# Attention and two MoE layers on one core: raw weight pieces fetched apart from their conversion, and new places for the start-up's steps

## The chip, the cores and the metric

The program runs on one core of a Trainium2 chip. Its time is device microseconds (us) of one launch; lower is better. The core has five instruction engines, each of which takes its own queue in order: PE (TensorE: matmuls and transposes), DVE (VectorE), ACT (ScalarE), POOL (GpSimd) and SP (SyncE, which issues most of the DMAs here). SBUF is the on-chip memory, PSUM the accumulators that PE writes.

## The reference

Attention with four batches, eight heads, 576 tokens and head size 64; then a dense MoE layer on the 2304 tokens; then a layer of eight experts of which each token takes one.

```
scores = q @ k.T / 8                       # (4, 8, 576, 576)
heads 0..3: keep 0 <= i - j < 32;  heads 4..7: keep j <= i and j % 32 == i % 32
x = softmax(scores) @ v                    # -> (2304, 512)
h = x @ w_in                               # 512 -> 1024      (float64 weights)
solu = h * softmax(h)
y = layernorm(solu) * g_ln @ w_out         # 1024 -> 512      (float64 weights)
logits = y @ w_gate + modality_bias[modality_id]
e = argmax(logits);  out = softmax(logits)[e] * (relu(y @ w1[e]) @ w2[e])
```

## The kernel before, in words

The big matmuls split each float32 operand into a high part and a low rest and add three products. So each weight matrix stands in SBUF twice: `winH` and `winL` for `w_in`, `woH` and `woL` for `w_out`.

`w_in` and `w_out` arrive as float64. A **raw piece** is 128 rows of 512 such numbers (512 KB); there are eight of either matrix. One piece is converted in steps. A multiplication of its upper words gives `mag` (on ACT or on POOL, by the letter in `MAG_ON`). Three operations on DVE put the bits of a float32 together in `wf` (lines 246, 247, 249); with a `P` in `SIGN_ON`, POOL clears all but the sign bit first (line 242) and two operations on DVE are enough (243, 249). ACT copies the high part (257 for `w_in`, 269 for `w_out`), and DVE or POOL subtracts it to get the low part (258; 272 and 274 by `LOW_ON`). A piece of `w_out` then goes through `fuse_gate`: four transposes of `wf` (`pt`) and four small matmuls with the gate's weights (`pg`). When all eight are done, `column_sums` runs 32 matmuls on them.

Attention works on pairs of heads, sixteen in all, with batch 0's strided pairs first. A pair has four **units**. A unit of a strided pair in batch 0 (`compact`) goes: 16 small matmuls into the PSUM tile `S`; DVE adds the mask, takes the maximum, subtracts it; ACT takes the exponential; DVE sums and inverts (396); four POOL operations spread the result into a zeroed tile (`spread`, line 399); PE transposes it (`pP`, 510), ACT copies that (`pT`, 518), and after two units PE multiplies with the values (`po`, 526), which ACT and DVE split into `xTH` and `xTL`. Units 0 to 7 are of this kind; units 8 to 15, two local pairs, take another way with the normalisation `ex` on POOL (462). Before a pair's units its q and k are transposed on PE (`ptq`) and copied by ACT (`qT`, `kz`).

`attention_slots` cuts this into numbered slots; `take(n)` emits them up to number n. Ahead of the first MoE tile the program takes some 72 slots, with the conversions of `w_in` set between them by `W_IN_AT`. Within the eighteen tiles of the first MoE layer, `between` emits conversions of `w_out` (`W_OUT_AT`), gates (`GATE_AT`) and slots of the next batch (`TAKES`). A tile has `moe_a` (24 matmuls of 512 columns into two `ph` tiles, then the exponential `e` on ACT and `so` on DVE, line 643, which frees `ph`) and, one tile later, `moe_b`. A tile scheduler orders each engine's queue from that. All buffers of a tag rotate: an instruction that fills one waits for the last reader of what it held. `raw` has three buffers, and q and k of the pairs share three of the tag `qk`.

Of the kernel before, what the change touches and what calls it, by code (L numbers as in the profile page):

```python
# [28 lines left out]
def tile_attention_moe_moe2(  # L29
# [56 lines left out]
    TAKES = [0, 5, 1, 8, 1, 0, 7, 0, 0, 4, 2, 0, 3, 0, 6, 0, 1, 0, 4, 0, 3, 0, 6, 0, 5, 0, 7, 0, 2, 1, 0, 3, 4, 2, 5, 0, 3, 0, 2, 0, 0, 0, 5, 0, 7, 0, 0, 4, 1, 0, 5, 2, 0, 0, 1, 1, 4, 0, 5, 0, 4, 0, 2, 0, 2, 0, 6, 4, 2, 2, 3, 0, 3, 0, 4, 0, 0, 1, 2, 1, 0, 0, 12, 0, 8, 3, 1, 0, 2, 2, 0, 0, 4, 0, 4, 0, 3, 0, 6, 0, 1, 1, 4, 0, 0, 0, 0, 0, 0]  # L86
# [46 lines left out]
    def flip_tile(out_, in_, eye):  # L133
        return nc.tensor.transpose(out_, in_, eye)  # L134
# [5 lines left out]
    def warm(n):  # L140
        wide = ident.bitcast(mybir.dt.bfloat16)
        for _ in range(n):
            nc.tensor.matmul(warm_out, wide[:, 0:P], wide, start=True, stop=True)
# [6 lines left out]

    def build_masks():
        nc.gpsimd.memset(rebias, 2.0 ** -112)
        nc.gpsimd.memset(zeros, 0.0)
        rank = mp.tile([P, 1], I32, name="rank", tag="e")
        rankf = mp.tile([P, 1], F32, name="rankf", tag="e")
# [6 lines left out]
        place = mp.tile([P, WIN], F32, name="place", tag="so")  # L162
        early = mp.tile([P, WIN], F32, name="early", tag="so")
# [10 lines left out]
        apart = mp.tile([SP_, SP_], I32, name="apart", tag="so")  # L174
# [7 lines left out]
    def build_consts():  # L182
# [17 lines left out]
        rows = mp.tile([NTILE, 2, P], F32, name="rows", tag="so")  # L200
# [29 lines left out]
    def f64_piece(src, tm, tw, by_act, sgn="D"):  # L230
        raw = rawp.tile([P, 512, 2], I32, name="raw")
        nc.sync.dma_start(raw, src)
        hi, lo = raw[:, :, 1], raw[:, :, 0]
        mag = mp.tile([P, 512], F32, name="mag", tag=tm)
        w = mp.tile([P, 512], F32, name="wf", tag=tw)
        wi = w.bitcast(I32)
        if by_act:
            nc.scalar.activation(mag, hi.bitcast(F32), AF.Copy, scale=REBIAS)
        else:
            nc.gpsimd.tensor_tensor(mag, hi.bitcast(F32), rebias.to_broadcast([P, 512]), ALU.mult)  # L240
        if sgn == "P":
# [11 lines left out]
    def prep_w_in(i):  # L253
        c, hf = divmod(i, 2)
        cs = slice(hf * 512, hf * 512 + 512)
        w = f64_piece(w_in32[:, c, cs], "e", "so", MAG_ON[i] == "A", SIGN_ON[i])
        nc.scalar.copy(winH[:, c, cs], w)
        nc.vector.tensor_tensor(winL[:, c, cs], w, winH[:, c, cs].bitcast(F32), ALU.subtract)

    def prep_w_out(f):  # L260
        w = f64_piece(w_out32[:, f], "nH", "yt", MAG_ON[8 + f] == "A", SIGN_ON[8 + f])
# [79 lines left out]
    def transpose_part(b, hp, part, qn, kn, qT, kT):  # L341
# [7 lines left out]
        if long:  # L349
            across = flat.rearrange("c (p i) -> c p i", i=n)  # L350
            for i in range(n):
                for j in range(2):
                    rows = slice(j * D, j * D + D)
                    nc.tensor.matmul(
                        pt[rows, i] if part < 2 else across[rows, :, i],
                        src[:, j, u, i * D:(i + 1) * D], ident[:QT, :QT], start=True, stop=True)
# [9 lines left out]
        for rows, dst in dsts:  # L366
            dst = dst[rows, u * (S // 2):(u + 1) * (S // 2)]
            if long and part < 2:
                nc.scalar.copy(
# [1061 lines left out]
```

## Time and profile before

| | |
|---|---|
| median of 3 runs | 648.2 us (645.41 to 650.27) |
| the profiled execution: its time, its span | 643.14 us, 641.4 us |
| PE busy | 602.3 us (94%) |
| DVE, ACT, POOL busy | 346.8, 286.3, 151.5 us |
| mean granted PE clock | 0.986 |

The span runs from the first to the last instruction. A matmul's row lasts longer than the time until the next may start, so a busy PE says that work was there; what an instruction costs in a row of the same is read from the distance of two starts. The profile gives for each wait the event that ended it. Attention of batch 0 fills about the first 66 us of the span; then the tiles of the first MoE layer follow, with attention of the other batches between them, and the experts from about 340 us on.

### The profile page before, as it was taken

The page shows a single profiled execution, that of the slowest core. Times are in us where ns is not written, and L with a number is a line of the kernel's source. Part 1 is how long each engine was busy: PE and PEld are TensorE (multiplying, and loading weights), DVE is VectorE, ACT ScalarE, POOL GpSimd, SP SyncE. Part 2 cuts the span into 40 slices and gives each one's busy share as a digit, 9 for nine tenths or more (in the row PEclk, how much of TensorE's full clock was granted, in tenths as well). Part 3 has the DMA queues.
Part 4 walks back from the last instruction along what each step waited for, and adds up shares of the span by engine and source line. Part 5 has one row for each costly group of instructions (what it writes and reads, how often), then busy time and mean ns, then how long its engine had stood idle before and what let it go on. Part 6 is the DMA issues. An engine that isn't in the chain of part 4 may idle for free. (4 is left out here: it accounts for less than half of the span.)

```text
span 641.4 us, 14417 instructions
## 1 busy us (share of the span) xinstructions
PE 602.3 (94%) x5546; PEld 535.7 (84%) x5546; DVE 346.8 (54%) x1020; ACT 286.3 (45%) x673; POOL 151.5 (24%) x223
## 2 busy tenths in 40 slices
PE   5887989999999999999999999999899999999992
PEld 4765777998889988978889999989798888899891
DVE  4865887488556775577488743217264643120120
ACT  3646675555554566557265522124335352221210
POOL 3652432112112352011023312310111203112101
PEclk9997989999999999999999999999999999999997
DMA  8676630224312123110044301445455453012010
GB/s 224 189 179 171 158 108 19 54 56 117 82 55 57 53 59 108 37 36 17 18 149 148 98 19 34 112 158 158 143 165 198 147 187 104 17 50 66 33 34 25
DMA packets 48387, 61.64 MB, mean 96 GB/s; under 512 B 29313, under 2 KB 32923, under 8 KB 48285
## 3 DMA queue, kind: packets, MB, share of 16 engines
q1 hardware_dynamic: 41421, 44.09, 24.7%
q0 software_dynamic: 4272, 11.57, 5.8%
q10 hardware_dynamic: 2592, 4.72, 2.0%
q8 instruction: 52, 0.85, 0.6%
q14 instruction: 50, 0.41, 0.2%
HBM read 48.40 MB, written 10.26 MB: 91 GB/s over the span
## 5 line engine op out<-in xcount | busy, mean ns | idle before, releaser
L1015 PE MATMUL py<-w2H,winL 128*128 128x512 f32 x288 | 92.1, 395 | 0.0
L1055 PE MATMUL pf<-xTL,w1H 128*128 128x256 f32 x288 | 81.8, 284 | 1.0 <-DVE xTL L994 1.0
L1055 PE MATMUL pf<-xTH,w1H 128*128 128x256 f32 x288 | 82.0, 285 | 0.0
L1055 PE MATMUL pf<-xTH,w1L 128*128 128x256 f32 x288 | 81.4, 283 | 0.0
L1062 DVE SCALAR_TENSOR_TENSOR winL<-pf,winL 128x512 fp32r<-128x512 f32 x36 | 24.9, 692 | 95.9 <-ACT winL L1061 95.8
L628 PE MATMUL ph<-winH,xTH 128*128 128x512 f32 x144 | 58.8, 408 | 4.2 <-DVE so L643 3.1
L1015 PEld LDWEIGHTS py<-w2H,winL 128*128 128x128 f32 x288 | 53.4, 188 | 10.5
L1061 ACT ACTIVATE winL<-pf 128x512 fp32r<-128x512 f32 x36 | 21.6, 599 | 87.5 <-PE pf L1055 87.5
L1055 PEld LDWEIGHTS pf<-xTL,w1H 128*128 128x128 f32 x288 | 56.2, 195 | 1.9 <-DVE xTL L994 1.6
L628 PE MATMUL ph<-winL,xTH 128*128 128x512 f32 x144 | 57.6, 400 | 0.0
L1055 PEld LDWEIGHTS pf<-xTH,w1H 128*128 128x128 f32 x288 | 56.1, 195 | 1.0 <-issue 0.5
L628 PE MATMUL ph<-winH,xTL 128*128 128x512 f32 x144 | 56.9, 401 | 0.0
L1055 PEld LDWEIGHTS pf<-xTH,w1L 128*128 128x128 f32 x288 | 56.2, 195 | 0.0
L1021 POOL DMA_INDIRECT out_dram<-yo,idx x14 | 14.1, 1007 | 142.6 <-ACT yo L1020 124.4
L687 PE MATMUL pa<-woH,nH 128*128 128x264 f32 x144 | 42.3, 293 | 1.0 <-ACT nH L676 1.0
L687 PE MATMUL pa<-woH,nL 128*128 128x264 f32 x144 | 42.6, 296 | 0.0
L687 PE MATMUL pb<-woH,nH 128*128 128x256 f32 x144 | 41.2, 286 | 0.0
L687 PE MATMUL pb<-woH,nL 128*128 128x256 f32 x144 | 41.0, 284 | 0.0
L687 PE MATMUL pa<-woL,nH 128*128 128x264 f32 x144 | 40.9, 284 | 0.0
L687 PE MATMUL pb<-woL,nH 128*128 128x256 f32 x144 | 40.8, 283 | 0.0
L462 POOL TENSOR_TENSOR ex<-ex,rd 72x288 f32<-72x288 f32 (+2 forms) x32 | 22.3, 696 | 70.9 <-DVE rd L457 44.4
L628 PEld LDWEIGHTS ph<-winH,xTH 128*128 128x128 f32 x144 | 27.4, 191 | 10.6 <-DVE so L643 4.5
(288 smaller groups left out, 1535.7 us busy)
## 6 DMA issues: line engine op xcount, KB each, us to landing
raw<-in_moe_w_dram SPq DMA_DIRECT2D x36, 512.0 KB
y_d<-yt ACTq DMA_DIRECT2D x18, 256.0 KB
raw<-in_moe_w_in_dram SPq DMA_DIRECT2D x8, 512.0 KB
raw<-in_moe_w_out_dram SPq DMA_DIRECT2D x8, 512.0 KB
qn<-in_q_dram SPq DMA_DIRECT2D x8, 288.0 KB
kn<-in_k_dram SPq DMA_DIRECT2D x8, 288.0 KB
vn<-in_v_dram SPq DMA_DIRECT2D x8, 288.0 KB
qn<-in_q_dram SPq DMA_DIRECT2D x16, 144.0 KB
```

The source lines that it names most:

```text
L462: nc.gpsimd.tensor_tensor(ex, ex, rd.unsqueeze(2).to_broadcast([nq, nt, nk]), ALU.mult)
L628: nc.tensor.matmul(ph, a[:, c, ts_], w[:, c, cs], start=n == 0, stop=n == 3 * KD - 1)
L687: nc.tensor.matmul(p, a[:, f], w[:, f, cols], start=n == 0, stop=n == 3 * KF - 1)
L1015: nc.tensor.matmul(p, a[:, f, s], x, start=n == 0, stop=n == 3 * KF - 1)
L1021: nc.gpsimd.indirect_dma_start(out=out[:, :], out_offset=indirect(idx[:, col, 2:3].bitcast(U32)), in_=o, in_offset=None, bounds_check=NT - ...
L1055: mm = nc.tensor.matmul(p[:, u], a[:, c, fs], x[:, c], start=n == 0, stop=n == 3 * KD - 1)
L1061: last[0] = (nc.scalar.activation(hH[:, f2s], p, AF.Relu), nc.vector.scalar_tensor_tensor(hL[:, f2s], p, 0.0, hH[:, f2s].bitcast(F32), ALU ...
L1062: nc.vector.scalar_tensor_tensor(hL[:, f2s], p, 0.0, hH[:, f2s].bitcast(F32), ALU.max, ALU.subtract))
```

## The change

Fetching and converting are two functions now. `fetch_w_in` and `fetch_w_out` only issue the DMA of a raw piece, at slots `FETCH_IN_AT` and `FETCH_OUT_AT`; `prep_w_in` and `prep_w_out` convert what has been fetched. Two of the eight raw pieces of `w_in` go into buffers of the tag `nH`, which stand unused then. So do pair 1's keys (`KN1_HOME`), which took a `qk` buffer that pair 0's q held. The pieces are converted in the order `IN_ORDER`, at other slots; seven of the eight conversions of `w_out` stand ahead of the first MoE tile in program order. The letters that set the engines are new: of `w_in`, five `mag`, one sign step and two low parts go to POOL (before: none); of `w_out`, four low parts (before two) and two sign steps (before one). `take` calls `warm` with 1 and 11 unused matmuls at slots 32 and 58; the start had eight already. `TAKES` differs in its first sixty entries. `mm`, `note`, `moe_a`'s split into `hidden` and `gate_hidden`, `moe_a_two` and the list `pending` change nothing with the numbers as set. The diff, cut:

```diff
-    MAG_ON = "AAAAAAAAPPPAAPPA"
-    SIGN_ON = "DDDDDDDDDDDDDDDP"
-    LOW_ON = "DPDDPDDD"
-    W_IN_AT = [3, 5, 8, 26, 35, 39, 52, 66]
-    W_OUT_AT = [1, 1, 2, 3, 3, 3, 4, 6]
-    GATE_AT = [1, 2, 2, 3, 3, 4, 4, 6]
+    MAG_ON = 'AAPPPPPAPAPPAAPP'
+    SIGN_ON = 'DDDPDDDDDPDDPDDD'
+    W_IN_LOW = 'PDDDPDDD'
+    LOW_ON = 'DDPDPPDP'
+    KN1_HOME = True
+    IN_ORDER = [0, 3, 7, 1, 6, 2, 4, 5]
+    FILL = {58: 11, 32: 1}
+    W_IN_AT = [1, 1, 4, 22, 23, 26, 27, 36]
+    CONSTS_AT = 70
+    RAW_HOME = 'rrrnrrnr'
+    FETCH_IN_AT = [1, 1, 1, 1, 1, 1, 2, 2]
+    FETCH_OUT_AT = [22, 40, 62]
+    OUT_AHEAD = 2
+    W_OUT_AT = [70, 70, 70, 70, 71, 72, 72, 100]
+    GATE_AT = [70, 70, 70, 100, 100, 100, 100, 100]
...
+    def fetch_w_in(i):
+        c, hf = divmod(IN_ORDER[i], 2)
+        if RAW_HOME[i] == "r":
+            raw_in[i] = rawp.tile([P, 512, 2], I32, name="raw")
+        else:
+            raw_in[i] = mp.tile([P, 512, 2], I32, name="raw", tag=dict(n="nH", y="yt")[RAW_HOME[i]])
+        nc.sync.dma_start(raw_in[i], w_in32[:, c, hf * 512:hf * 512 + 512])
...
-    def f64_piece(src, tm, tw, by_act, sgn="D"):
-        raw = rawp.tile([P, 512, 2], I32, name="raw")
-        nc.sync.dma_start(raw, src)
+    def f64_piece(raw, tm, tw, by_act, sgn="D"):
...
-        nc.vector.tensor_tensor(winL[:, c, cs], w, winH[:, c, cs].bitcast(F32), ALU.subtract)
+        low = nc.gpsimd if W_IN_LOW[i] == "P" else nc.vector
+        low.tensor_tensor(winL[:, c, cs], w, winH[:, c, cs].bitcast(F32), ALU.subtract)
...
+        if n_ == 1 and KN1_HOME:
+            kn = mp.tile([QT, 2 * SG * D], F32, name="kn", tag="nH")
...
             next(slots, None)
+            if taken in FILL:
+                warm(FILL[taken], True)
             taken += 1
```

Three places show what the scheduler made of it.

POOL, from the spread of unit 0 on, before (`zrow` and `tabi` are constants for later):

```order
L399 TENSOR_TENSOR spread_112<-exc_126,rd 32x72 x4
L399 TENSOR_TENSOR spread_112<-exc_128,rd 32x72 x4
L399 TENSOR_TENSOR spread_113<-exc_130,rd 32x72 x4
L399 TENSOR_TENSOR spread_113<-exc_126,rd 32x72 x4
L399 TENSOR_TENSOR spread_112<-exc_128,rd 32x72 x4
L399 TENSOR_TENSOR spread_112<-exc_130,rd 32x72 x4
L193 MEMSET zrow 1x512
```

and now:

```order
L457 TENSOR_TENSOR spread_112<-exc_126,rd 32x72 x4
L292 TENSOR_TENSOR mag<-raw,rebias 128x512
L312 TENSOR_TENSOR winL<-wf,winH 128x512
L292 TENSOR_TENSOR mag<-raw,rebias 128x512
L457 TENSOR_TENSOR spread_112<-exc_128,rd 32x72 x4
L295 TENSOR_TENSOR raw<-raw,zeros 128x512
L457 TENSOR_TENSOR spread_113<-exc_130,rd 32x72 x4
L292 TENSOR_TENSOR mag<-raw,rebias 128x512
L457 TENSOR_TENSOR spread_113<-exc_126,rd 32x72 x4
L292 TENSOR_TENSOR mag<-raw,rebias 128x512 x2
L457 TENSOR_TENSOR spread_112<-exc_128,rd 32x72 x4
L312 TENSOR_TENSOR winL<-wf,winH 128x512
```

Conversion steps of `w_in` stand between the spreads; up to unit 7's spread a sign step and a `mag` of `w_out`, a `mag` of which stood there before too, follow.

ACT, from the exponential of unit 8 to that of unit 10, with the copies `pT` of units 6 and 7, before:

```order
L447 ACTIVATE ex<-ex,nb 128x64 x4
L534 CAST xTH<-po 128x72x4
L518 COPY pT<-pP 72x288
L369 COPY qT<-ptq 128x288
L238 ACTIVATE mag<-raw 128x512
L518 COPY pT<-pP 72x288
L447 ACTIVATE ex<-ex,nb 128x64 x5
```

and now:

```order
L503 ACTIVATE ex<-ex,nb 128x64 x4
L584 CAST xTH<-po 128x72x4
L570 COPY pT<-pP 72x288
L428 COPY qT<-ptq 128x288
L570 COPY pT<-pP 72x288
L431 COPY kz_119<-ptq 64x288 x2
L503 ACTIVATE ex<-ex,nb 128x64 x5
```

The `mag` of a `w_out` piece ahead of unit 7's `pT` is gone from this place.

PE, between the second and the third MoE tile (`pt` and `pg` are the gates of `w_out`, `ph` the tile's matmuls), before:

```order
L286 MATMUL pg<-wg,wt 128x8 x4
L134 MATMUL ptq<-ident,qn 128x72 x4
L489 MATMUL po_1363<-pT,vn 64x32 x4
L489 MATMUL bank<-pT,vn 64x32 x4
L489 MATMUL po_1363<-pT,vn 64x32 x4
L489 MATMUL bank<-pT,vn 64x32 x4
L134 MATMUL ptq<-ident,qn 128x72 x4
L134 MATMUL pt<-ident,wf 128x128 x4
L628 MATMUL ph<-winH,xTH 128x512
```

and now:

```order
L668 MATMUL ph<-winH,xTL 128x512
L152 MATMUL pt<-ident,wf 128x128 x4
L342 MATMUL pg<-wg,wt 128x8 x4
L152 MATMUL ptq<-ident,kn 128x96 x3
L342 MATMUL pg<-wg,wt 128x8 x4
L152 MATMUL ptq<-ident,kn 128x96 x3
L774 MATMUL pa<-woH,onesR 128x264
L774 MATMUL pa<-woL,onesR 128x264
```

All eight gates are done there, and fourteen matmuls of `column_sums` (two of them shown) stand ahead of the third tile's first `ph`; before, five gates were done and none of the column sums.

## Rows read from the trace of the kernel before

**Rows 1.** Windows of the span: busy us and instructions of each engine, PE clock, DMA.

```profile
10.00:20.00 10.00, 4.79 (x123) 4.09 (x122) 6.09 (x20) 4.73 (x11) 2.69 (x6) 1.00 0.90 260
13.00:45.00 32.00, 25.63 (x384) 21.28 (x384) 26.21 (x76) 18.10 (x45) 20.42 (x37) 1.00 0.70 183
57.00:64.00 7.00, 6.49 (x151) 4.76 (x141) 3.88 (x13) 5.29 (x20) 0.62 (x1) 1.00 0.41 87
66.00:117.00 51.00, 48.02 (x516) 40.17 (x516) 40.22 (x119) 33.06 (x88) 15.53 (x21) 0.97 0.36 92
77.00:91.00 14.00, 12.40 (x111) 10.74 (x112) 13.37 (x35) 10.08 (x28) 6.77 (x7) 1.00 0.43 129
117.00:330.00 213.00, 209.36 (x2270) 186.69 (x2269) 143.03 (x520) 115.55 (x312) 43.16 (x66) 1.00 0.22 59
```

**Rows 2.** Waits of PE, 0 to 110 us: total us, times, longest.

```profile
PE po L526 <- ACT pT L518: 3.3, 1, 3.3
```

**Rows 3.** Timeline: start, length, engine, work [idle before <- what ended it].

```profile
12.42 0.66 ACT L238 ACTIVATE mag<-raw 128x512 f32<-128x512 f32 x1 [3.50 <-DMA raw<-in_moe_w_in_dram]
...
14.77 2.47 POOL L399 TENSOR_TENSOR spread<-exc,rd 32x72 f32<-32x72 f32 x4 [8.11 <-DVE exc L388]
...
18.08 0.71 PE L134 MATMUL ptq<-ident,kn 72*128 72x72 f32 x4 [2.59 <-DMA kn<-in_k_dram]
```

**Rows 4.** Timeline, unit 7: spread, transposes (`pP`), `po`; on ACT, unit 8's exponential.

```profile
42.66 2.21 POOL L399 TENSOR_TENSOR spread<-exc,rd 32x72 f32<-32x72 f32 x4
...
46.17 1.06 ACT L447 ACTIVATE ex<-ex,nb 128x64 f32<-128x64 f32 x4 [3.61 <-DVE nb L445]
...
47.96 1.17 PE L510 MATMUL pP<-ident,spread 128*72 128x72 f32 x8 [1.00 <-ACT pT L518]
...
52.08 0.66 ACT L238 ACTIVATE mag<-raw 128x512 f32<-128x512 f32 x1 [3.98 <-DMA raw<-in_moe_w_out_dram]
...
53.08 1.23 PE L526 MATMUL po<-pT,vn 72*64 72x72 f32 x16 [3.30 <-ACT pT L518]
```

**Rows 5.** Groups by form, 13 to 45 us: count | busy us, mean ns | idle before.

```profile
L258 DVE TENSOR_TENSOR winL<-wf,winH 128x512 fp32r<-128x512 f32 x8 | 6.0, 745 | 3.5 <-ACT winH L257 3.5
L246 DVE TENSOR_SCALAR wf<-mag 128x512 int32<-128x512 int32 x9 | 4.1, 461 | 5.3 <-ACT mag L238 3.6 <-POOL mag L240 1.7
```

**Rows 6.** Groups by form, POOL, 66 to 113 us.

```profile
L272 POOL TENSOR_TENSOR woL<-wf,woH 128x256 fp32r<-128x256 f32 x4 | 2.8, 731 | 0.8 <-ACT woH L269 0.8
...
L242 POOL TENSOR_TENSOR raw<-raw,zeros 128x512 f32<-128x512 f32 x1 | 1.1, 1057 | 1.1 <-ACT mag L238 1.1
```

**Rows 7.** Timeline of DVE, two conversion steps in a row.

```profile
38.12 0.69 DVE L247 SCALAR_TENSOR_TENSOR wf<-raw,wf 128x512 int32<-128x512 int32 x1
38.72 0.69 DVE L258 TENSOR_TENSOR winL<-wf,winH 128x512 fp32r<-128x512 f32 x1
```

**Rows 8.** Timeline of POOL and DVE at 50 us.

```profile
50.46 1.10 POOL L240 TENSOR_TENSOR mag<-raw,rebias 128x512 f32<-128x512 f32 x1 [0.81 <-DMA raw<-in_moe_w_out_dram]
50.69 1.41 DVE L249 SCALAR_TENSOR_TENSOR wf<-raw,wf 128x512 int32<-128x512 int32 x1
```

**Rows 9.** Timeline of PE at the second and third tile's first matmuls.

```profile
77.29 0.50 PE L628 MATMUL ph<-winH,xTH 128*128 128x512 f32 x1 [0.97 <-DVE so L643]
...
90.75 0.77 PE L134 MATMUL pt<-ident,wf 128*128 128x128 f32 x4 [1.14 <-ACT qT L372]
91.95 0.79 PE L628 MATMUL ph<-winH,xTH 128*128 128x512 f32 x1 [0.43 <-DVE so L643]
...
94.64 0.40 PE L628 MATMUL ph<-winH,xTH 128*128 128x512 f32 x1
...
95.79 0.40 PE L628 MATMUL ph<-winH,xTL 128*128 128x512 f32 x1
```

**Rows 10.** Timeline of PE: the start's unused matmuls, and a wait at 63 us.

```profile
2.32 1.89 PE L143 MATMUL bank<-ident 128*128 128x256 bf16 x8 [2.32 <-POOL ident masks.py:199]
...
64.53 0.47 PE L134 MATMUL ptq<-ident,qn 96*128 96x96 f32 x3 [1.03 <-ACT kz L372]
```

More of the change, by code (lines that the diff above doesn't have):

```diff
@@ L138, in tile_attention_moe_moe2, with warm @@
     bankS, bankO = bank[:, 0:5 * WIN], bank[:, 5 * WIN:8 * WIN]
-    def warm(n):
+    last_mm = [None]
+    def warm(n, after=False):
         wide = ident.bitcast(mybir.dt.bfloat16)
         for _ in range(n):
-            nc.tensor.matmul(warm_out, wide[:, 0:P], wide, start=True, stop=True)
+            mm = nc.tensor.matmul(warm_out, wide[:, 0:P], wide, start=True, stop=True)
+            if after and last_mm[0]:
+                queue_after(mm, last_mm[0])
+            last_mm[0] = mm
     def queue_after(later, earlier):
@@ L149, in queue_after, with note, behind_newest @@
             reason="issue order")
+    newest = {}
+    def note(x):
+        newest[x.ins.engine] = x
+    def behind_newest(x):
+        if ANCHOR and x.ins.engine in newest:
+            queue_after(x, newest[x.ins.engine])
     def build_masks():
@@ L353, in transpose_part @@
                     rows = slice(j * D, j * D + D)
-                    nc.tensor.matmul(
-                        pt[rows, i] if part < 2 else across[rows, :, i],
-                        src[:, j, u, i * D:(i + 1) * D], ident[:QT, :QT], start=True, stop=True)
+                    mm(pt[rows, i] if part < 2 else across[rows, :, i],
+                       src[:, j, u, i * D:(i + 1) * D], ident[:QT, :QT])
         else:
@@ L645, in moe_a, with moe_a_two @@
         return so, e, s2, a2
+    def moe_a(t, front, between):
+        mx = st.tile([P, 2], F32, name="hmx")
+        late_ = done_att and t % 2
+        hs = []
+        for hf in range(2):
+            kw = dict(tag=("S", "o")[hf], bufs=1) if late_ else dict(tag="h")
+            hs.append(hidden(t, hf, mx=mx, step=between, **kw))
+            if hf == 0:
+                front()
+                between(1)
+        return gate_hidden(hs, mx)
+    def moe_a_two(between):
+        mx = [st.tile([P, 2], F32, name="hmx") for _ in range(2)]
+        hs = [[], []]
+        for hf in range(2):
+            for t in range(2):
+                hs[t].append(hidden(t, hf, "hy"[t], mx[t], between))
+                between()
+        return [gate_hidden(h, m) for h, m in zip(hs, mx)]
     pow_ = [None]
@@ L690, in moe_b @@
                     between(f == KF - 1)
+                if f == KF - 1 and p is pa:
+                    then()
         yt = mp.tile([P, DM], F32, name="yt")
@@ L1164, in tile_attention_moe_moe2 @@
     state = None
+    pending, stats, made = [], {}, {}
     done_att = False
```

250 lines of the change are left out of this document (147 added, 103 removed).

## The prediction

> **What bounds the kernel now.** I read the windows first. From 117 us on PE is at work in 209.36 of 213 us, between 66 and 117 us in 48.02 of 51, both with hardly any loss of clock [rows 1]. So nothing that DVE, ACT or POOL are spared after 66 us is worth anything unless PE waits for it there. From 13 to 45 us no engine is full: DVE 26.21 of 32 us, ACT 18.10, POOL 20.42 [rows 1]. That stretch is a chain that goes round the engines, with raw pieces from DMA (260 GB/s at a share of 0.90 between 10 and 20 us) feeding it from the side. A change can therefore move the end in two ways: it lets the chain of the start reach the first tiles earlier or later, and then every us counts once; or it removes PE's waits between 66 and 117 us. PE's list of waits says which ones are large: the longest is `po` of unit 7, 3.3 us behind an ACT copy [rows 2].
>
> The sum stands against the profiled execution, 643.14 us (span 641.4, 1.7 around it). The median is 0.8% higher; a difference of some us carries over as it is.
>
> **Term A, the start up to `po` of unit 7.** Before, pair 1's keys waited for their buffer behind raw pieces: the transposes `ptq<-kn` waited 2.59 us and began at 18.08, and the first `mag` on ACT waited 3.50 us for its raw piece, until 12.42 [rows 3]. Now q and k of both pairs go first and the raw pieces follow. That isn't a gain of 2.59 us. The first transposes of a spread (`pP`) can't begin before the first spread ends, 14.77 + 2.47 = 17.24, near the same time [rows 3]. And pair 1's k, 2 × 144 × 1 KB or 0.295 MB, now lies ahead of the first raw piece: at 260 GB/s that is 1.1 us by which the first `mag` comes later, and what hangs on it.
>
> How does unit 7's `po` come at 53.08? Its spread is over at 42.66 + 2.21 = 44.87. Unit 8's exponential stands ahead of unit 6's `pT` on ACT and waits for DVE until 46.17; then `pT`, then unit 7's `pP` at 47.96, which is over at 49.13. Its `pT` could follow at once, but a `mag` of `w_out` stands ahead of it on ACT and waits 3.98 us for its raw piece; `po` waits 3.30 us for that [rows 4]. This `mag` leaves the place now. So without any other change `po` would come at 53.08 − 3.30 = 49.8, and the path is: unit 8's DVE step (46.2) plus 3.6, or unit 7's spread plus 1.7 (`pP` 1.17, `pT` 0.34 from 53.08 − 52.08 − 0.66, and the steps between), whichever is later.
>
> What is added to POOL up to unit 7's spread: five `mag` and two sign steps at 1.06 (the sign step's 1057 ns), two low parts of 512 columns at 2 × 0.731 [rows 6], in all 7.4 + 2.9 = 10.3 us. POOL idles 11.6 of the 32 us [rows 1], so there is room, but only just: were it never idle after its first spread (14.77 + 1.1 = 15.9), unit 7's would end at 15.9 + 20.4 + 10.3 = 46.6. DVE loses two low parts and a step or two, and gets two pieces of `w_out` ahead of unit 7's reciprocal: twice a step like line 249 (0.69 long), twice one with two operands (between 0.46 and 0.69, taken 0.6), an addition for unit 8 (0.46 at most), less one low part at 0.69 [rows 5, 7]: 2.35 us. By that way the spread ends at 44.87 + 1.1 + 2.35 = 48.3.
>
> Then there is what POOL and DVE do to each other. At 50 us a POOL `mag` of 1.10 us and a step of line 249 began 0.23 us apart: the DVE step took 1.41 us [rows 8], where two such steps in a row take 0.69 and start 0.60 apart [rows 7]. That is 0.72 more. The Trainium skill, "SBUF — State Buffer", section "Who interferes with whom", has a rule for it: DVE and GpSimd share one pair of ports, and when a DVE instruction with two inputs in SBUF meets a GpSimd instruction that reads SBUF, the one that came first holds the pair for its whole length. The trace agrees in that row, 1.41 us against 0.69; by the rule alone, every one of the new POOL steps would stop a DVE step that comes while it runs, which speaks against moving them. Ten POOL steps of this form stand ahead of unit 7's spread in the new order (six `mag`, two sign steps, two low parts). If none meets a DVE step the addition is 0; if all do, 10 × 0.72 = 7.2. Some stand where DVE waits for just that POOL step: of line 246's 5.3 us of waits before, 1.7 were for the one `mag` on POOL [rows 5]. I take six meetings with half of 0.72 each, 2.2 us. So the spread ends at 50.5 and `po` comes at 52.2, 0.9 us earlier than before. **A = −0.9.** Its ends: with POOL never idle and no meeting, unit 8's step at 46.2 lets `po` come at 49.8 or 50.0, −3.1; with all ten, the spread ends at 55.5 and `po` comes at 57.2, +4.1.
>
> **Term B, the tiles from 66 to 117 us.** At the second tile's first `ph` PE waits 0.97 us for `so`; ahead of the third's it waits 1.14 for ACT and 0.43 for `so`, and then the clock is low for a moment: six matmuls take 94.64 − 91.95 = 2.69 us where the next five take 95.79 − 94.64 = 1.15, 0.23 each, so the loss is 2.69 − 6 × 0.23 = 1.3 [rows 9]. Now three more gates, at 0.77 us for the four transposes [rows 9] and some tenths for the small matmuls each, and 14 matmuls of the column sums stand ahead of the third tile's first `ph`. PE needs this work anyway, so it fills the wait: 1.14, 0.43 and the 1.3 of low clock go. **B = −2.8** (2.87, rounded down). The 0.97 stays: DVE has one more conversion ahead of that `so`, which takes what the longer filling gives. Low end: it goes too, −3.8. High end: DVE is busy 13.37 of 14 us from 77 to 91 [rows 1], so what comes on top there is delay. One more conversion is 0.46 + 0.69 + 0.745 = 1.9 [rows 5, 7], and four more halves of low parts on POOL (0.731 each [rows 6]) may hold a DVE step for a third of their time, 1.0: +2.9 with nothing filled.
>
> **Term C, the unused matmuls.** Eight of them took 1.89 us at the start, 0.236 each with the low clock [rows 10]. Eleven more are 2.6 us at that level and 1.3 at the high one. They stand behind slot 58, near 63 us, where the granted clock is 1.00 from 57 to 64 us, so they can't raise it; and PE waits 1.03 us there for an ACT copy [rows 10], which covers most of 1.3. **C = +0.3**, with 0 and +1.6 as ends (2.6 less the wait). The one at slot 32 falls into idle time.
>
> **The rest** (the new `TAKES` after 117 us, another order of the constants, the sign step moved in `w_out`): 0, since PE has only 213 − 209.36 = 3.6 us without work in all that stretch and none of it is named by these edits; 1 us either way.
>
> Sum: −0.9 − 2.8 + 0.3 = −3.4 us. From 643.14 that is 639.7; from the median, **644.8 us**, within 1%, which is about what a measurement of this kernel can tell from no change.
>
> **Rivals.** *The chain shortens fully* (faster): POOL takes the new steps in its idle time, no DVE step is held, and the raw waits of 3.98 and 0.97 are both gone: −3.1 − 3.8 + 0 = −6.9, 641.3. For it: POOL's 11.6 us of idle time, and that DVE waited 5.3 us for `mag`, whose raw pieces are now fetched earlier, into two more buffers. Against: the row of 1.41 us. *POOL and DVE hold each other* (slower): the spread of unit 7 then ends at 55.5, and the same happens to the low parts beside the first tiles: +4.1 + 2.9 + 0.3 = +7.3, 648.2 + 7.3 = 655.5. It decides from the point where A eats up the other two terms, +2.5 on `po`, that is a spread of unit 7 that ends after 53.9. For it: each new POOL `mag` is 1.06 us long where ACT took 0.66, and units wait for POOL's spreads in the same queue. *Nothing comes of it*: the wait of 3.98 us for a raw piece leaves unit 7's `pT` but comes up at another step, since the bytes and the DMA share (0.70 from 13 to 45) are the same, and B's waits turn up one tile later: about 0, 648.2.
>
> **How the numbers follow.** The sum as it stands 0.45 (by itself 641 to 649, from the middle halves of A and B), the full gain 0.25, mutual holding 0.18, nothing 0.12. Faster by over 1% (under 641.7) comes from half of the full gain and from the lower fourth of the forecast's own spread (its A and B ends): 0.13 + 0.12 = 0.25. Slower by over 1% (over 654.7) needs most of the holding, 0.15 with something from the unbounded rest. The range leaves out the far parts of both: from 637, four below the full gain for the rest's 1 us and the spread of the runs themselves (2.8 below the median), to 655, where holding is about reached.
>
> **What would show it.** Right for A: the first `mag` about 1 us later than 12.42, `ptq<-kn` without a DMA wait, unit 7's spread over near 50.5, its `po` near 52.2 and waiting for POOL or DVE rather than for a raw piece behind ACT. Wrong: a spread that ends before 48.5 or after 54, or a new raw wait on POOL's queue. Line 302's steps (249 before) beside POOL steps of 512 columns should show lengths between 0.7 and 1.4; if they are all 0.69, the holding is wrong. Right for B: no wait over 0.4 ahead of the third tile's first `ph` and a clock of 1.00 from there on; wrong: a wait for `so` that is longer at the second tile. Right for C: eleven matmuls in 1.3 us with a PE wait near them gone. After 117 us the two traces should run at a constant distance; if they don't, the rest was not 0, and the prediction is wrong where I looked least.

## The result, and the profile after

The changed kernel takes 650.26 us (median of 20 runs, 647.91 to 655.75) against 645.24 us (20 runs, 642.20 to 650.27): a ratio of 1.0082, interval 1.006 to 1.0104. It is slower by 5.0 us, where 3.4 us faster was forecast. The median of 648.2 us, from which the forecast started, was that of three runs; twenty runs, those three among them, give 645.24.

The profiled execution took 655.75 us, its span is 653.9 us. A second trace of each kernel gave 654.27 and 644.48 us. So both traces of the changed kernel lie above its median, by 4.0 and 5.5 us, and both of the kernel before below its own, by 2.1 and 0.8; what they show in excess of 5 us has to be read with care. The beginning of each tile's first `ph` agrees within 0.7 us between the two traces of either kernel.

Windows of the changed kernel (columns as in [rows 1]):

```profile
13.00:45.00 32.00, 19.90 (x313) 16.62 (x313) 26.39 (x65) 14.35 (x36) 26.28 (x37) 1.00 0.62 187
45.00:55.00 10.00, 10.00 (x122) 7.92 (x121) 7.23 (x19) 4.00 (x12) 4.43 (x11) 1.00 0.57 160
55.00:65.00 10.00, 10.00 (x154) 7.91 (x151) 5.06 (x16) 6.26 (x21) 3.50 (x5) 1.00 0.91 183
66.00:117.00 51.00, 48.50 (x556) 42.02 (x557) 35.06 (x99) 34.08 (x94) 16.41 (x23) 0.93 0.36 90
117.00:330.00 213.00, 210.53 (x2293) 186.40 (x2292) 145.07 (x513) 117.37 (x316) 44.99 (x68) 1.00 0.21 57
```

From 13 to 45 us POOL is now as busy as DVE, 26.28 of 32 us (before 20.42 [rows 1]), PE did less (19.90 against 25.63), and from 45 to 65 us PE is never without work. PE's list of waits up to 110 us, its largest entries and the one ahead of the second tile:

```profile
PE pP L156 <- ACT pT L570: 3.5, 2, 2.2
PE pP L156 <- POOL spread L457: 3.4, 2, 2.7
...
PE pg L342 <- DVE woL L330: 1.2, 1, 1.2
```

The wait of `po` for the raw piece [rows 2, 4] and that of `ptq` for `kn` [rows 3] are gone, and PE waits for POOL's spreads and ACT's copies of them (`pT`) instead. Timeline, the first steps that answer to [rows 3]:

```profile
13.84 0.66 ACT L290 ACTIVATE mag<-raw 128x512 f32<-128x512 f32 x1 [3.02 <-DMA raw<-in_moe_w_in_dram]
...
16.21 2.31 POOL L457 TENSOR_TENSOR spread<-exc,rd 32x72 f32<-32x72 f32 x4 [9.56 <-DVE rd L454]
...
18.58 1.26 PE L156 MATMUL pP<-ident,spread 128*72 128x72 f32 x8 [2.72 <-POOL spread L457]
```

The first `mag` is 1.4 us later, the first spread too, and PE's first `pP` stands at 18.58 where pair 1's keys held PE until 18.08 before: what the keys gain is swallowed, as forecast. In the second trace of the changed kernel the first spread begins at 17.64. So the first spread itself moves by over a us from trace to trace, and how far unit 7's spread lies behind it is the steadier measure: 35.5 us in both traces of the changed kernel, 30.1 and 29.0 in those of the kernel before.

From its first to its sixth spread POOL has no wait now. The fourth and the fifth:

```profile
28.68 1.04 POOL L292 TENSOR_TENSOR mag<-raw,rebias 128x512 f32<-128x512 f32 x1
29.69 2.29 POOL L457 TENSOR_TENSOR spread<-exc,rd 32x72 f32<-32x72 f32 x4
32.05 2.50 POOL L292 TENSOR_TENSOR mag<-raw,rebias 128x512 f32<-128x512 f32 x2
34.52 2.46 POOL L457 TENSOR_TENSOR spread<-exc,rd 32x72 f32<-32x72 f32 x4
```

Unit 7 (answers to [rows 4]):

```profile
50.23 1.44 POOL L457 TENSOR_TENSOR spread<-exc,rd 32x72 f32<-32x72 f32 x4 [1.89 <-DVE rd L454]
...
52.75 1.26 PE L156 MATMUL pP<-ident,spread 128*72 128x72 f32 x8
...
54.11 0.39 ACT L570 COPY pT<-pP 72x288 f32<-72x288 f32 x1 [1.55 <-PE pP L156]
...
54.30 1.23 PE L156 MATMUL ptq<-ident,kn 96*64 96x96 f32 x12
...
55.31 1.17 PE L156 MATMUL po<-pT,vn 72*64 72x72 f32 x16
```

The spread ends at 51.67 (before 44.87), and now PE's own queue lies between it and `po`: there is no wait in brackets at any of PE's rows. They run at the low clock (the 16 `po` take 1.17 us, and 0.67 at the high clock in a kernel shown below). Three transposes of q, and the first tile's first and third `ph`:

```profile
59.76 0.74 PE L152 MATMUL ptq<-ident,qn 96*128 96x96 f32 x3
...
64.15 0.80 PE L668 MATMUL ph<-winH,xTH 128*128 128x512 f32 x1
...
65.55 0.40 PE L668 MATMUL ph<-winH,xTL 128*128 128x512 f32 x1
```

The same three transposes in the kernel before:

```profile
57.35 0.47 PE L134 MATMUL ptq<-ident,qn 96*128 96x96 f32 x3
```

So PE came to its high clock (2.4 GHz) for good at 57 us there, after it had had it from 46.8 to 50.2, and at 65 us here. The first tile begins at 64.15 instead of 59.92: 4.2 us later. From there to the eighteenth tile (353.2 and 348.1) the two take 289.0 and 288.2 us.

The groups of DVE by form, 13 to 50 us, of the kernel before:

```profile
L249 DVE SCALAR_TENSOR_TENSOR wf<-raw,wf 128x512 int32<-128x512 int32 x9 | 6.2, 694 | 0.0
...
L391 DVE TENSOR_TENSOR exc<-exc,mx 128x72 f32<-128x72 f32 x7 | 1.9, 271 | 0.0
```

and of the changed one:

```profile
L302 DVE SCALAR_TENSOR_TENSOR wf<-raw,wf 128x512 int32<-128x512 int32 x10 | 8.6, 861 | 0.0
...
L449 DVE TENSOR_TENSOR exc<-exc,mx 128x72 f32<-128x72 f32 x7 | 4.3, 615 | 0.0
```

The same two operations last 167 and 344 ns longer: 10 x 0.167 + 7 x 0.344 = 4.1 us that DVE was held. The experiments tell below that this isn't the main thing that makes the start late.

### The profile page after: what moved, and what is told of

Its sections match the earlier page's. It is cut to its first block, busy times and chain, and to the rows that moved or that the text cites. A ratio compares the mean times of both kernels' runs of the same rounds, so it can differ in the third digit from the quotient of the medians.

```text
span 653.9 us, 14444 instructions
## 1 busy us (share of the span) xinstructions
PE 612.7 (94%) x5558; PEld 544.7 (83%) x5558; DVE 349.5 (53%) x1012; ACT 285.2 (44%) x670; POOL 162.0 (25%) x236
## 5 line engine op out<-in xcount | busy, mean ns | idle before, releaser
L1102 PEld LDWEIGHTS py<-w2H,winL 128*128 128x128 f32 x288 | 53.3, 188 | 10.5
L1142 PEld LDWEIGHTS pf<-xTL,w1H 128*128 128x128 f32 x288 | 56.2, 195 | 0.8 <-DVE xTL L1081 0.5
L1142 PEld LDWEIGHTS pf<-xTH,w1L 128*128 128x128 f32 x288 | 56.2, 195 | 0.0
L496 POOL TENSOR_TENSOR ex<-ex,mx 72x288 f32<-72x288 f32 (+2 forms) x24 | 18.0, 748 | 69.5 <-DVE mx L492 41.8
```

What stands on the lines that cost most here:

```text
L496: eng.tensor_tensor(ex, ex, mx.unsqueeze(2).to_broadcast([nq, nt, nk]), ALU.subtract)
L1102: nc.tensor.matmul(p, a[:, f, s], x, start=n == 0, stop=n == 3 * KF - 1)
L1142: mm = nc.tensor.matmul(p[:, u], a[:, c, fs], x[:, c], start=n == 0, stop=n == 3 * KD - 1)
```

## The experiments

All are the changed kernel but for the lines shown, except where the kernel before is named. The ratio is to the kernel before, run on the same chip (its medians were 643.8 to 645.4 us). Up to the first tile five things are read from the timelines: where unit 7's spread ends, how long that is after the first spread began, where unit 7's `po` begins, where the first tile's first `ph` begins, and how PE's matmuls tell its clock. Then the starts of the sixth and eighteenth tile. A median is that of 6 to 20 runs; the places are those of one trace.

| kernel | spread ends | after the first | `po` | tile 1 | tile 6 | tile 18 | median | ratio (interval) |
|---|---|---|---|---|---|---|---|---|
| before | 44.9 | 30.1 | 53.1 | 59.9 | 166.6 | 348.1 | 645.2 | |
| changed | 51.7 | 35.5 | 55.3 | 64.2 | 172.5 | 353.2 | 650.3 | 1.0082 (1.006 to 1.0104) |
| nofill | 51.9 | 35.5 | 54.8 | 62.0 | 174.4 | 354.6 | 653.0 | 1.0125 (1.0082 to 1.0168) |
| warm30 | 51.4 | 35.2 | 55.6 | 61.1 | 174.8 | 355.1 | 654.4 | 1.0139 (1.0098 to 1.0179) |
| places | 52.1 | 35.8 | 55.2 | 62.1 | 174.0 | 354.6 | 654.2 | 1.0130 (1.0096 to 1.0164) |
| inmags | 46.7 | 31.5 | 50.0 | 56.4 | 165.7 | 346.0 | 645.0 | 1.0012 (0.998 to 1.0044) |
| inletters | 45.6 | 29.5 | 49.2 | 55.0 | 168.1 | 348.3 | 644.7 | 0.9995 (0.9964 to 1.0025) |
| letters | 46.4 | 30.7 | 52.3 | 59.3 | 171.6 | 352.6 | 651.9 | 1.0123 (1.009 to 1.0156) |
| early | 46.8 | 31.2 | 53.3 | 60.9 | 173.0 | 354.0 | 650.4 | 1.0094 (1.006 to 1.0129) |
| before_mags | 46.0 | 31.8 | 55.8 | 64.6 | 172.8 | 354.1 | 654.3 | 1.0168 (1.0136 to 1.0199) |

**The steps of w_in on POOL.** One kernel takes all of them back (inletters), one only the five `mag` (inmags):

```diff
-    MAG_ON = 'AAPPPPPAPAPPAAPP'
+    MAG_ON = 'AAAAAAAAPAPPAAPP'
-    SIGN_ON = 'DDDPDDDDDPDDPDDD'
+    SIGN_ON = 'DDDDDDDDDPDDPDDD'     # inletters only
-    W_IN_LOW = 'PDDDPDDD'
+    W_IN_LOW = 'DDDDDDDD'            # inletters only
```

> The changed kernel with all of w_in's conversion steps back on ACT and DVE (letters of before), everything else as changed. Theory one (the POOL steps delay the units' spreads and hold DVE): unit 7's spread ends near 46 instead of 51.7, the first tile begins near 60 to 61 instead of 64.2, and 3 to 4 of the 5 us are gone. Theory two (the start is late because PE works at its low clock until 65 us while the kernel before has the high one from 57): the spread comes earlier, but the first tile no more than 1 us earlier, and at most 1 us is gone.

> The changed kernel with only the five mag of w_in back on ACT; its sign step and two low parts stay on POOL, which leaves 4.4 of the 9.3 us that the new w_in steps took there. If POOL's queue and its holding of DVE delay the units in proportion to POOL's time, unit 7's spread ends near 48.5 (51.7 in the changed kernel, 45.6 with all letters of w_in back), the first tile begins near 58, and the time lies about halfway, near 647. If it is the two long low parts and the sign step that hold DVE, nearly nothing is gained: spread near 50.5, time near 649.

With the five `mag` back on ACT the loss is gone. Timeline of POOL in inmags, the end of unit 7's spread:

```profile
45.22 1.44 POOL L457 TENSOR_TENSOR spread<-exc,rd 32x72 f32<-32x72 f32 x4 [1.87 <-DVE rd L454]
```

and of PE, unit 7's `po` and the first tile:

```profile
49.99 0.67 PE L156 MATMUL po<-pT,vn 72*64 72x72 f32 x16
...
56.40 0.50 PE L668 MATMUL ph<-winH,xTH 128*128 128x512 f32 x1
```

The spread ends 5.0 us earlier for 5 x 1.13 us taken off POOL; 1.0 of that is there before the first spread, which begins at 15.19. Counted from it, the `mag` cost 4.0 us (35.5 against 31.5), and the two low parts and the sign step, 4.4 us of POOL in the changed kernel's groups, 2.0 more (31.5 against 29.5), though in inletters the scheduler also sets one `w_out` piece less ahead of unit 7's reciprocal on DVE. So POOL's time alone isn't the measure, and the expectation by proportion was wrong. It may be a matter of whom the work was taken from: ACT, from which the `mag` came, was busy 18.10 of 32 us [rows 1]; DVE, from which the others came, 26.21, so that what POOL's queue lost there DVE got back. That is argued, not shown.

Is it POOL's queue or the holding of DVE? The same two groups of DVE in inmags:

```profile
L302 DVE SCALAR_TENSOR_TENSOR wf<-raw,wf 128x512 int32<-128x512 int32 x10 | 9.5, 954 | 0.0
...
L449 DVE TENSOR_TENSOR exc<-exc,mx 128x72 f32<-128x72 f32 x7 | 2.7, 386 | 0.0
```

By the same reckoning DVE was held 10 x 0.260 + 7 x 0.115 = 3.4 us there, only 0.7 less than in the changed kernel (1.6 less with the eight steps of line 299, 444 against 562 ns), and yet the spread comes 4.0 us earlier. So the holding is real, but most of what the `mag` cost is something else. What differs is the queue. In inmags POOL waits for work again ahead of the fifth spread:

```profile
29.93 2.16 POOL L457 TENSOR_TENSOR spread<-exc,rd 32x72 f32<-32x72 f32 x4 [0.66 <-ACT exc L451]
```

In the changed kernel all five `mag` stand ahead of that spread, without a wait. The distance of the two kernels is 1.0 us at the first spread, 4.6 at the fifth and 4.9 to 5.7 behind it.

**The other direction.** The five `mag` alone, put into the kernel before:

```diff
-    MAG_ON = "AAAAAAAAPPPAAPPA"
+    MAG_ON = "AAPPPPPAPPPAAPPA"
```

> The kernel before with one thing of the change: the same five mag of w_in on POOL. If POOL's mags ahead of the spreads are what delays the start (they held unit 7's spread back by 5.0 us in the changed kernel), unit 7's spread ends 3 to 5 us after 44.9, the first tile begins near 62 to 64, and the time is 2 to 4 us over the kernel before. If the delay needs the changed kernel's places of w_in, the spread ends within 1 us of 45 and the time is the same within 1 us.

It is slower by ten us, twice what the changed kernel loses, but not as expected: the spread moves by only 1.1 us. What moves is the raw piece that unit 7's `pT` waits for. ACT in this kernel:

```profile
54.76 0.66 ACT L238 ACTIVATE mag<-raw 128x512 f32<-128x512 f32 x1 [5.51 <-DMA raw<-in_moe_w_out_dram]
```

It landed at 52.08 before [rows 4], 2.7 us earlier, and `po` moves by the same 2.7. Of these, 1.0 us lies ahead of the issue of this piece (47.98 against 47.01), which would fit raw buffers that come free later; the other 1.7 lie between issue and landing, and their cause is open. The clock rises at 66.4 instead of 57.0, and that adds 2.0 from `po` to the first tile. So POOL's `mag` cost the first tile 4.7 us here and 7.8 in the changed kernel (64.2 less inmags' 56.4), but not in the same way: in the changed kernel by the spreads, here by a raw piece. Of the ten us here six stand at the eighteenth tile; the rest comes behind it.

**The clock at the start.** Three kernels have the changed kernel's start, and its spread within 0.5 us: without the unused matmuls (nofill), with eight more ahead of unit 7 (warm30), and with `w_out`'s places as before (places).

```diff
-    FILL = {58: 11, 32: 1}
+    FILL = {}                        # nofill
+    FILL = {58: 11, 32: 1, 30: 8}    # warm30
-    W_OUT_AT = [70, 70, 70, 70, 71, 72, 72, 100]
+    W_OUT_AT = [101, 101, 102, 103, 103, 103, 104, 106]    # places
-    GATE_AT = [70, 70, 70, 100, 100, 100, 100, 100]
+    GATE_AT = [101, 102, 102, 103, 103, 104, 104, 106]     # places
```

> The changed kernel without its twelve unused matmuls. If they only add PE time, the eleven of them, which took 1.2 us at the high clock behind a wait of 0.75 us, are saved: about 1.2 us less than the changed kernel, and the first tile still begins near 64 us. If they hold the clock up for the tiles behind them, the second tile gets slower instead: 1 to 2 us more. If the theories of the start (POOL holding the units, or the clock staying low until 65 us) are right, the excess of 5 us over the kernel before stays at 4 or more.

> The changed kernel with eight more unused matmuls ahead of unit 7, where PE waits for 2.2 us. Theory two (low clock): matmuls at the high level show before 57 us, unit 8's to 11's work takes half the time and the first tile begins near 61 instead of 64.2: 2 to 3 us less. Theory one (POOL and DVE set the pace): nothing gained, the first tile at 64 to 66 us, the time the same or up to 2 us more.

> The changed kernel with w_out converted and its gates put at the places of the kernel before, between the first tiles. Theory one or two (the loss is in the start, up to the first tile): the first tile begins within 1 us of 64, and the time stays 4 to 5 us over the kernel before. Theory three (the gates ahead of the second tile, with PE's waits of 0.5 and 1.2 us there and a low clock from 82 to 89 us, cost the time): 2 to 3 us less.

The granted clock rises at 53.7 us in warm30, 59.6 in nofill, 54.2 in places (low again from 61.0 to 64.4) and 65.3 in the changed kernel (60.9 in its second trace), and the first tile follows: 61.1, 62.0, 62.1, 64.2, with `po` in the same place within 0.8 us. Where the clock is high for most of the way (inletters, inmags, warm30) 9.4 to 9.7 us lie between unit 7's spread and the first tile; in the changed kernel 12.5. So the low clock cost some 3 us of its start. Its second trace shows that the share varies: from `po` to the first tile it took 8.8 us where the clock rose at 65.3 and 6.9 where it rose at 60.9, with the same queues (kernel before: 6.8 and 7.5). So warm30 did to the first tile what the theory of the clock said, but its time rose where 2 to 3 us less were expected, and that of places rose as well: all three kernels end later than the changed one. Each takes 3.5 to 5.3 us more than it between the first and the sixth tile. Nor does taking the unused matmuls out free their time, since the scheduler sets what stands behind them in another order: nofill waits 6.4 us for `so`.

**The lead that doesn't last.** inletters begins its first tile 4.9 us before the kernel before and has nothing left of that at the sixth. Its windows from 65 to 95 us:

```profile
65.00:75.00 10.00, 8.30 (x52) 7.37 (x51) 9.96 (x22) 6.91 (x19) 5.03 (x5) 0.88 0.62 182
75.00:85.00 10.00, 10.00 (x96) 8.13 (x95) 8.17 (x23) 6.41 (x16) 5.85 (x8) 0.61 0.43 112
85.00:95.00 10.00, 10.00 (x70) 8.67 (x60) 4.90 (x13) 4.03 (x11) 2.37 (x4) 0.66 0.03 7
```

DVE is full, PE waits, the clock falls: 0.61 and 0.66 over 20 us is some 15 us at the low level. Four kernels tried to keep the lead, each on inletters or (alllow) on inmags:

```diff
+    FILL = {58: 11, 32: 1, 70: 12}                         # inl_fill
+    LOW_ON = 'PPPPPPPP'                                    # alllow
+    W_OUT_AT = [101, 101, 102, 103, 103, 103, 104, 106]    # lead_places
+    GATE_AT = [101, 102, 102, 103, 103, 104, 104, 106]     # lead_places
+    FILL = {}                                              # lead_places
+    W_OUT_AT = [70, 70, 101, 101, 102, 103, 104, 106]      # lead_half
+    GATE_AT = [100, 101, 102, 103, 103, 104, 104, 106]     # lead_half
```

lead_places has the `TAKES` of the kernel before as well.

> The kernel with w_in's letters put back, and twelve unused matmuls more in the wait of 1.2 us ahead of the second tile's gate. In the kernel without them the first tile began at 55, 5 us ahead of the kernel before, and the lead was gone by 130 us; between 72 and 93 us it worked 17 us at the low clock. If the low clock is what eats the lead, and PE's waits bring it, the low stretch shrinks, and the time falls by 3 to 6 us, to about 640. If it is the conversion of w_out on DVE that eats it, the twelve matmuls are hidden or cost up to 1.3 us: 645 to 646.

> The changed kernel with the five mag of w_in on ACT (which gave 645.0) and all low parts of w_out on POOL. If DVE's shortage between 60 and 80 us (9.96 of 10 us busy) brings the waits ahead of the second tile and the low clock behind them, DVE gets 8 halves less of some 0.47 us, the second tile begins 2 to 4 us earlier, the low stretch shrinks and the time falls to 641 to 643. If POOL's low parts hold DVE as they run, or POOL now comes last, it stays at 645 or rises.

> The changed kernel with w_in's letters back on ACT and DVE, w_out's places and the slots per call of the kernel before, and no unused matmuls; the letters of w_out stay the changed kernel's. The first tile should begin near 55 (no raw wait ahead of unit 7's pT on ACT, no POOL steps ahead of the spreads). If the seven conversions of w_out ahead of the first tile, with DVE full between 65 and 75 us, ate that lead by waits and a low clock, the tiles now run as in the kernel before (288 us from the first to the eighteenth), the eighteenth begins near 343 and the time is 640 to 641, under both kernels. If the lead is lost whatever w_out's places are, the tiles take 292 to 293 us and the time is 644 to 646.

> The changed kernel with w_in's letters back, and two conversions of w_out ahead of the first tile, the others from the first tile on, one or two at a time; the rest as changed. If DVE's load ahead of the second tile is what ate the lead, the low clock behind it shrinks and the time is 641 to 643; if the later conversions are waited for instead, or the lead is lost anyway, 645 or more.

| kernel | tile 1 | tile 6 | tile 18 | median | ratio (interval) |
|---|---|---|---|---|---|
| inl_fill | 55.5 | 167.6 | 348.8 | 651.1 | 1.0093 (1.0058 to 1.0128) |
| alllow | 57.3 | 168.5 | 348.7 | 648.0 | 1.0058 (1.0033 to 1.0082) |
| lead_places | 56.2 | 168.4 | 349.7 | 646.2 | 1.0010 (0.9985 to 1.0035) |
| lead_half | 54.1 | 167.9 | 348.5 | 650.7 | 1.0078 (1.0045 to 1.0111) |

None keeps it. Windows of inl_fill:

```profile
65.00:75.00 10.00, 9.46 (x78) 8.32 (x78) 9.96 (x22) 6.76 (x20) 5.03 (x5) 1.00 0.60 179
75.00:85.00 10.00, 9.63 (x126) 8.10 (x125) 8.79 (x24) 6.72 (x17) 6.08 (x8) 1.00 0.43 116
85.00:95.00 10.00, 7.31 (x39) 6.08 (x38) 7.34 (x25) 7.26 (x19) 4.14 (x6) 0.79 0.03 7
```

The unused matmuls do hold the clock up to 85 us, and the third tile comes 6.8 us earlier than in inletters (91.6 against 98.4); then PE waits instead, and the sixth tile comes 0.5 us earlier. In seven kernels, before among them, whose first tile begins between 54.1 and 59.9, the sixth begins between 165.7 and 168.5, whatever the first did; letters, with 59.3 and 171.6, is the exception. Where the lead goes can be read from PE's window between these two tiles, in the kernel before, the changed one, inletters and lead_half:

```profile
59.92:166.63 106.71, 102.44 (x1205) 89.99 (x1202) 79.41 (x258) 64.75 (x174) 26.33 (x39) 0.98 0.34 85
64.15:172.54 108.39, 105.49 (x1210) 93.09 (x1209) 78.34 (x249) 65.11 (x172) 28.49 (x42) 0.97 0.32 83
55.01:168.08 113.07, 109.95 (x1208) 96.61 (x1209) 79.73 (x254) 65.74 (x175) 29.41 (x43) 0.92 0.32 82
54.15:167.85 113.70, 106.62 (x1208) 93.78 (x1209) 77.99 (x254) 66.35 (x174) 29.08 (x43) 0.95 0.33 82
```

In the last three the work of PE is the same, 1208 instructions. inletters idles about as long as the changed kernel, 3.1 against 2.9 us, but its clock is low for 17.1 us and not 6.8, and PE is busy 4.5 us longer with the same matmuls. lead_half, 5.3 us longer than the changed kernel, is idle for 7.1 us, 4.2 of them more than there. So the lead goes into the low clock in the one, and mostly into waits in the other. DVE is full from 65 to 75 us in the windows of inletters and inl_fill, but over the whole stretch it is busy for only 78 to 80 of 107 to 114 us. Which of its steps comes too late wasn't tried by itself, and moving all low parts to POOL made it no better (alllow is slower than the kernel before). Left open is why inl_fill and lead_half end at 651 in the median, and alllow at 648, with an eighteenth tile that stands where that of inletters does.

**The rest of the letters, and the early fetch alone.** letters puts all letters of the kernel before back, `w_out`'s too; early does that and also takes back `w_out`'s places, `TAKES` and the unused matmuls:

```diff
+    MAG_ON = 'AAAAAAAAPPPAAPPA'      # letters, early
+    SIGN_ON = 'DDDDDDDDDDDDDDDP'     # letters, early
+    W_IN_LOW = 'DDDDDDDD'            # letters, early
+    LOW_ON = 'DPDDPDDD'              # letters, early
+    FILL = {}                        # early
```

> The changed kernel with all letters of the kernel before, those of w_out too: three low parts of w_out go back from POOL to DVE and one sign step moves. If POOL's low parts beside the first tiles hold DVE there, it is 1 to 2 us faster than with w_in's letters alone (643); if DVE is short of time there, the new ones are the better ones and it is 1 to 3 us slower (646 to 648). The first tile begins near 55 either way.

> The changed kernel with all letters, w_out's places, the slots per call and no unused matmuls as in the kernel before: what is left of the change is the early fetch, the buffer for pair 1's keys and the new order and places of w_in. If the start's gain of 5 us (first tile near 55 instead of 59.9) is theirs and the tiles then go as in the kernel before, 168.7 us from the first tile to the tenth, the time is 640 to 641, under the kernel before by 4 to 5. If the lead is lost behind w_out's conversion again, it is within 1 us of 645.

Both expectations failed, of the start (59.3 and 60.9, not 55) and of the time (651.9 and 650.4). With the old letters of `w_out` the wait for a raw piece is back ahead of unit 7's `pT`. ACT in letters:

```profile
51.30 0.66 ACT L290 ACTIVATE mag<-raw 128x512 f32<-128x512 f32 x1 [3.62 <-DMA raw<-in_moe_w_out_dram]
```

`po` comes at 52.3 instead of 49.2 and the first tile 4.3 us later. So it is the letters of `w_out`, and by this row that of a `mag` (its three strings weren't tried apart), not the early fetch, that removed this wait, and the early fetch with pair 1's keys in another buffer brings the first tile no earlier (60.9 against 59.9).

**The same kernels again**, for a second trace:

> The changed kernel a second time, unchanged, for its trace. If the late rise of the clock (65 us) is what this start brings, it comes within some us of 65 again and the first tile near 64; if it falls by chance, it can come anywhere from 53 to 65 as in its three variants with the same start (53.7, 54.2, 59.6), and the first tile begins at 61 to 62. Unit 7's spread ends within 0.5 us of 51.7 in either case, and the 18th tile begins 4 to 6 us after 348.

> The kernel before a second time, unchanged, for its trace. Unit 7's spread ends within 0.5 us of 44.9 and po waits some 3 us for the raw piece again; the first tile begins at 58 to 61 by where the clock rises; the 18th tile begins within 2 us of 348. Behind it no piece of code differs from the changed kernel, so what differs there by several us from its first trace is what varies from run to run.

Changed: spread 53.1, first tile 63.7, eighteenth 352.6, 654.27 us. Before: 43.9, 60.0, 348.0, 644.48 us. Both spreads miss what was expected of them, by 1.4 and 1.0 us; the changed kernel's first spread began 1.4 us later, too. The distance at the eighteenth tile is 4.6 us, and 5.1 in the first pair. Behind that tile the work is the same, 1846 instructions of PE in either kernel, yet from it to the last transposes `pn` the changed kernel takes 33.9 us on the mean of its two traces and the kernel before 29.7. Timeline of POOL there, in the changed kernel:

```profile
357.39 0.96 POOL L826 DMA_INDIRECT tab_d<-entry,rpos  x1 [3.51 <-DMA tab_d<-entry,rpos]
359.76 0.96 POOL L826 DMA_INDIRECT tab_d<-entry,rpos  x1 [1.41 <-DMA tab_d<-entry,rpos]
360.74 0.57 POOL L724 TENSOR_TENSOR rstd<-rstd,mhalf 128x1 f32<-128x1 f32 x1
```

of DVE:

```profile
361.34 0.16 DVE L726 TENSOR_TENSOR sc<-rstd,rs 128x1 f32<-128x1 f32 x1 [3.59 <-POOL rstd L724]
```

and of PE:

```profile
367.03 0.36 PE L750 MATMUL pa<-woH,nH 128*128 128x264 f32 x1 [1.60 <-DVE LG L759]
...
369.49 0.42 PE L750 MATMUL pa<-woH,nL 128*128 128x264 f32 x1
```

A chain of scattered writes, each waiting 1.4 to 4.3 us for the one before to land, stands ahead of `rstd` on POOL. The last of them began 6.6 and 6.2 us after the eighteenth tile in the changed kernel's traces, 3.9 us in both of the kernel before, and PE then waits and works at the low clock for a while (0.42 us for a row of 0.28 at other times). In the traces of the other kernels it is 3.3 to 6.6 us, and where it is late that stretch is long. How often it is late in runs without a trace isn't known.

## Why the prediction was wrong

In short: the forecast counted POOL's new steps as free but for their holding of DVE, and they delay the spreads in POOL's own queue; it had no term for PE's queue behind the last spread, nor for the clock; and what it gained between the tiles came back as other waits.

**What bounds the kernel** held in part. PE is at work nearly all the time from 66 us on, as the forecast said. But "then every us counts once" isn't so: 4.2 us at the first tile and 5.1 at the eighteenth look like it, while inletters' first tile came 4.9 us earlier than that of the kernel before and its eighteenth 0.2 later, and early's came 1.0 later and its eighteenth 5.9. What the clock and PE's waits take between the first and the sixth tile is as large as the shift of the start.

**Term A** (forecast −0.9 at `po`, measured +2.2, and +4.2 at the first tile) is where it failed, in three steps.
- "I take six meetings with half of 0.72 each, 2.2 us. So the spread ends at 50.5": it ended at 51.7. That it is so near is luck, for two terms were wrong in opposite directions. POOL's ten steps were to cost 2.2 us, all of it by holding DVE, and nothing in POOL's queue ("there is room, but only just"). Five of them alone, the `mag`, cost 4.0 (changed 35.5 from the first spread, inmags 31.5), and most of that by the queue. All the rest, the two pieces of `w_out` on DVE among it, which were to cost 2.35, adds 1.4 (inmags 31.5, before 30.1). The holding itself was forecast rightly in kind, 4.1 us in two groups. By the rule of the Trainium skill, "SBUF — State Buffer", section "Who interferes with whom", a DVE instruction with two inputs in SBUF contends with a GpSimd instruction that reads SBUF, and the one that came first blocks the other; the trace agrees, 615 against 271 ns and 861 against 694 ns for two such operations. I counted the meetings of the long steps; the short ones with 72 columns, seven of them, paid more.
- "unit 7's spread plus 1.7": `po` came 3.6 us after it. I had taken PE as free there, because it waited in the trace before. At the low clock its work now filled it from 45 to 65 us without a gap, and what stands ahead of unit 7's `pP` and `po` in its queue set them. Late spreads aren't the reason: in inmags and inletters `po` comes 3.3 and 3.6 us after the spread as well. The other way to `po`, unit 8's step plus 3.6, was left at 46.2 + 3.6 although DVE's new work stands ahead of that step, too: its exponential began at 50.6, and 54.2 would have been the nearer forecast.
- That `po`'s shift carries over to the first tile: it grew by 2.0, since the clock rose at 65 and not at 57. In this the forecast had no term at all. Of the error of 5.1 us at the first tile 1.2 is the spread, 1.9 PE's queue and 2.0 the clock. In the second trace the same parts are 2.6, 1.9 and 0.1: the first spread began later there, and the clock rose ahead of the tile.

The parts of A that were right: the keys' gain is swallowed, and the raw wait of 3.98 us leaves unit 7's `pT` (by `w_out`'s letters, as letters showed). Without the five `mag` on POOL A would have been −3.1 at `po` (inmags, 50.0), the low end of the range.

**Term B** (forecast −2.8): the waits ahead of the third tile went, as forecast, and came back ahead of the second, for the gates stand there now. Windows of the changed kernel:

```profile
80.00:84.00 4.00, 2.80 (x18) 2.53 (x18) 3.97 (x10) 4.00 (x13) 2.16 (x3) 0.80 0.88 261
84.00:88.00 4.00, 4.00 (x48) 3.22 (x47) 4.00 (x15) 3.76 (x11) 1.91 (x3) 0.50 0.57 159
```

and its timeline of PE at the second tile:

```profile
82.04 1.57 PE L342 MATMUL pg<-wg,wt 128*128 128x8 f32 x8 [1.20 <-DVE woL L330]
85.91 0.79 PE L668 MATMUL ph<-winH,xTH 128*128 128x512 f32 x1
...
89.37 0.40 PE L668 MATMUL ph<-winH,xTL 128*128 128x512 f32 x1
```

The second tile begins at the low clock, and it lasts longer than the third's did in [rows 9]. From the first tile to the sixth the change costs 1.7 us (108.4 against 106.7), of which the eleven unused matmuls are 1.2: B is about +0.5, not −2.8, and +0.1 by the second traces.

**Term C** (+0.3): they took 1.2 us, at the high clock, behind a wait of 0.75, and nofill, without them, waits 1.0 and 0.5 us at this place. What they cost is near the forecast. **The rest** (0): right between the sixth and the eighteenth tile (180.7 against 181.5 us), wrong behind it in both traces.

The rival of mutual holding was nearer in its direction: it gave 655.5 and decided from a spread that ends after 53.9. The kernel got slower without reaching that point, and mostly not by the holding. This rival named the queue that all spreads share as a reason for itself, but put a price on the holding alone; the clock was in no rival. That 650.26 lies inside the range of 637 to 655 is no merit of the sum, whose direction was wrong.

## What to carry to other kernels

Work moved to an idle engine is free only if that engine has nothing of the chain queued behind it: five steps moved from ACT, which had time, to POOL, whose queue holds every unit's spread, put unit 7's spread 4 us and the first tile 7.8 us later than in the same kernel with these steps on ACT. A first tile that begins earlier is worth nothing until it is known what sets the later ones: here six kernels began it 2.6 to 5.8 us earlier than the kernel before, and none was measurably faster. Where PE's wait is removed, look at its clock too: the raw wait ahead of `po` went away, and the clock rose later; inletters' lead went into 17 us at the low clock with no more idle time than the changed kernel has.

## What had not been expected of the hardware

- PE worked from 45.5 to 65 us without a gap, on matmuls and transposes of mostly 32 to 96 columns, and stayed at the low clock until 65.3 us in one trace and 60.9 in the other of the same kernel; in variants with the same start it rose at 53.7, 54.2 and 59.6 us.
- The clock column shows 1.00 from 45 to 65 us there, although the three transposes at 59.76 took 0.74 us and not 0.47. Ahead of a trace's first recorded change of the clock the length of known matmuls tells the level, not the column.
- A DVE operation of 72 columns took 0.615 us in the mean of seven with POOL's steps of 512 columns in between, against 0.271. One of them, begun 0.12 us after a POOL sign step of 1.10 us, took 1.07 us: a short step can be held longer than it lasts.
